# Retention and gated feed-forward on one core: the second product with weights and moving operand exchanged, in four groups over 1024 tokens

## The chip, the core and the metric

The kernel runs on one NeuronCore of a Trainium2 chip. The core has a matrix engine (TensorE, in the profile PE; PEld is its loading of weights), VectorE (DVE), ScalarE (ACT), GpSimd (POOL) and SyncE (SP), on which this kernel issues its DMAs. Each engine has an instruction queue of its own and works through it in order; semaphores connect them. The metric is device time in microseconds (us), from runs on the chip.

## The reference

Inputs are `q`, `k`, `v` (4 batches, 8 heads, 768 steps, 64 dimensions), `w_in` (512 x 2048) and `w_out` (2048 x 512), all float32. First a retention: for each head a 64 x 64 state that decays by `gamma` and takes up one outer product a step.

```python
gamma = 1.0 - 2.0 ** (-5.0 - np.arange(H, dtype=np.float32))
for t in range(S):
    state = gamma[None, :, None, None] * state + np.einsum('bhd,bhe->bhde', k[:, :, t], v[:, :, t])
    y[:, :, t] = scale * np.einsum('bhd,bhde->bhe', q[:, :, t], state)
x = y.transpose(0, 2, 1, 3).reshape(B * S, H * D)      # 3072 tokens x 512
h = x @ w_in
g = h * np.clip(h + 3.0, 0.0, 6.0) / 6.0
out = g @ w_out                                        # 3072 x 512
```

## The kernel before

The program has two stages. **The first** makes `g`. Retention is done in rows of 128 tokens (`burst`, L237) as masked products plus a carried state. Its result `x` is multiplied with `w_in` in `mm1` (L363): one call takes one unit `u` of 512 tokens (`UT`) and one block `jj` of 128 features; 4 pieces of the inner dimension, 3 matmuls each (L368), with the weights from `w_in` and 512 columns of `x` moving. There are three because each float32 operand is kept as two tiles, a high part of type float32r and the rest (`split`, L136: ScalarE copies the high part, VectorE subtracts it), and three of the four cross products are added up. `mm1` ends with ScalarE (L372), VectorE (L373) and a store of `g` to DRAM, transposed, as `gd[jj // 2][:, jj % 2, tokens]` (L374). So `gd[j]` for j = 0..7 holds a pair of feature blocks, one of each half of the features, by 3072 tokens. `w_out` comes in and is made ready in `build_w2` (L165), piece by piece in the first stage; `w2c[j]` holds, for pair j, seven combinations of its four 128 x 256 blocks, each as high and low part and in two halves `h` of 128 output columns.

**The second stage** (L407 on) is the product with `w_out`, as a 2 x 2 block product with seven multiplications in place of eight. The four blocks of `g` are two halves of features (`f`) by two halves of tokens (`t`): a11 and a12 are the first tokens' halves of features, a21 and a22 the second tokens'. Products 1 to 7 take the left operands a11, a12, a12 - s2, a22, s1, s2 and a11 - a21, where s1 = a21 + a22 and s2 = s1 - a11. Twelve blocks `tb` of 256 tokens run one after the other; each has four chunks `cf` of two pairs. Per chunk two loads `gr` from `gd` on SP (L431), four sums of 256 elements on VectorE (L437 to L440), five splits, then 2 pairs x 7 products x 3 matmuls (L454): **weights are 128 tokens of the left operand, 256 columns of `w2c` move**, and the result lies with tokens on the partitions, in four PSUM banks `o`; two sets of banks alternate by block. At a block's end one ScalarE copy and seven VectorE combinations (L469) join the seven products, and one store (L481) writes 256 rows of `out`; the last block has four smaller stores (L485).

What sets the order: in the first stage TensorE's order is the order of the code (`manual_schedule`, L378, closed at L403). All else is ordered by a scheduler, by the order in the code and by what each instruction waits for. The first chunk's preparation has a raised priority and is done early; the other chunks of the first block are put behind the last `g` on VectorE (`issue_after(end)`, L428). Tiles come from pools; a tile taken again waits for its last users.

Of the kernel before, what the change touches and what calls it, by code (L numbers as in the profile page):

```python
# [9 lines left out]
F32 = mybir.dt.float32  # L10
# [14 lines left out]
LEFT = {1: 0, 2: 1, 3: 2, 4: 3, 5: 4, 6: 5, 7: 6}  # L25
# [4 lines left out]
def retention_ffn(ctx: ExitStack, tc: tile.TileContext, qkv, w_in, w_out, dvs, dqs, out, B, H, S, D):  # L30
# [7 lines left out]
    NT, DM = out.shape  # L38
# [47 lines left out]
    def nm(s):  # L86
        return f"{s}_{next(serial)}"
# [315 lines left out]
    order.close()  # L403
# [3 lines left out]
    sets = (late, ctx.enter_context(tc.tile_pool(name="gcpool", bufs=1, reuse_waits="tile")))  # L407
    gpool = ctx.enter_context(tc.tile_pool(name="gpool", bufs=2, reuse_waits="tile"))
# [4 lines left out]
    CF = 2  # L413

    for tb in range(NT // (2 * P)):
        t0 = tb * 2 * P
        banks = [ps_o[tb % 2].tile([P, 512], F32, tag=f"o{i}", name=f"o{tb}_{i}") for i in range(4)]
        acc = {}
        for b_, ids in enumerate(((1, 2), (6, 7), (5, 3), (4,))):
            for n, i in enumerate(ids):  # L420
                acc[i] = (banks[b_][:, n * HM : (n + 1) * HM], n == 0)
        for cf in range(NFP // CF):
            pool = sets[cf % 2]
            with ExitStack() as first:
                if tb == 0 and cf < 1:
                    first.enter_context(tc.high_priority())
                elif tb == 0:
                    first.enter_context(tc.issue_after(end))  # L428
                gv = pool.tile([P, CF, 2, 2, P], F32, tag="gr", name=f"gr{tb}_{cf}", bufs=2)
                for jj in range(CF):  # L430
                    nc.sync.dma_start(  # L431
                        out=gv[:, jj].rearrange("p f t n -> p f (t n)"),
                        in_=gd[cf * CF + jj][:, :, t0 : t0 + 2 * P],
                    )
                a11, a12, a21, a22 = gv[:, :, 0, 0, :], gv[:, :, 1, 0, :], gv[:, :, 0, 1, :], gv[:, :, 1, 1, :]
                sm = pool.tile([P, 4, CF, P], F32, tag="gsum", name=f"gsum{tb}_{cf}")
                dve_add(sm[:, 1], a21, a22)  # L437
                dve_sub(sm[:, 2], sm[:, 1], a11)
                dve_sub(sm[:, 3], a11, a21)
                dve_sub(sm[:, 0], a12, sm[:, 2])  # L440
                gc = pool.tile([P, 2, 7, CF, P], F32R, tag="gc", name=f"gc{tb}_{cf}")
                for i, src in ((0, a11), (1, a12), (3, a22)):
                    split(gc[:, 0, i], gc[:, 1, i], src)
# [115 lines left out]
```

## Time and profile before

| what | value |
|---|---|
| timed runs, median of 3 (lowest to highest) | 601.03 us (600.01 to 602.43) |
| profiled execution, first to last instruction | 597.6 us |
| median of the timed runs less that span | 3.4 us |
| mean granted clock of TensorE | 0.993 |
| matmuls, weight loads | 4988 each |
| read from HBM, written | 71.85 MB, 31.46 MB |

The time of a run is longer than the span of a profiled execution by what lies ahead of its first instruction and behind its last. The page of the profile gives, per engine, busy time as a share of the span, and the span in 40 slices, where a digit is the busy share in tenths. Matmuls overlap, so the mean duration of one is longer than the distance from one to the next. Groups of instructions are told by line, engine and operation, with `out<-in` by the program's names; behind the bar stand busy time, mean duration in ns, and the idle time ahead of them with what ended it. For one line the three numbers are the shortest, middle and longest duration in ns, then the first and last start in us. A DMA row gives its count, the size of one and the middle time from issue to landing.

### The profile page before, as it was taken

The numbers are of one execution on the slowest core, as the hardware profiler recorded it, in microseconds if no ns is written. First come the engines' busy times: TensorE is split into PE (matmuls) and PEld (weight loads), VectorE is DVE, ScalarE is ACT, GpSimd is POOL, SyncE is SP. The second block draws the span as 40 slices with busy tenths as digits, with TensorE's granted clock in tenths as the row PEclk, the third lists the DMA queues.
The fourth block names the chain that finished last, engine by engine and source line by source line (L and its number), as shares of the span: only waits on it lengthen the run. The fifth ranks groups of instructions, "written<-read, shape, count | busy, mean of one in ns | idle before, by whom it ended". The sixth has DMA issues, their size and how long they took to land.

```text
span 597.6 us, 12608 instructions
## 1 busy us (share of the span) xinstructions
PE 580.7 (97%) x4988; PEld 520.3 (87%) x4988; DVE 456.1 (76%) x961; ACT 253.3 (42%) x540; POOL 22.1 (4%) x27
## 2 busy tenths in 40 slices
PE   7698999999999999999999999999999999999997
PEld 6576888877888888888888889999999999999997
DVE  4889999999333797333356969998899889988983
ACT  5774544544222443222244634444444444444441
POOL 1001000010100010001000000000000000000000
PEclk9899999999999999999999999999999999999999
DMA  9976877566745468454244444443444344434411
GB/s 327 390 239 211 259 232 262 200 213 218 241 160 177 159 229 268 171 191 148 106 149 138 171 141 149 142 144 116 128 141 141 119 128 141 142 117 129 142 57 37
DMA packets 64731, 104.13 MB, mean 174 GB/s; under 512 B 5792, under 2 KB 30880, under 8 KB 64672
## 3 DMA queue, kind: packets, MB, share of 16 engines
q1 hardware_dynamic: 64528, 103.31, 51.7%
q8 instruction: 39, 0.64, 0.5%
q14 instruction: 20, 0.16, 0.1%
q10 hardware_dynamic: 144, 0.02, 0.0%
HBM read 71.85 MB, written 31.46 MB: 173 GB/s over the span
## 4 chain that ended last, share of the span: by engine, by line
PE 76%; DVE 17%; DMA 3%; issue 3%; SPq 1%; ACT 0%; DVEq 0%; ACTq 0%
PE o L454 40%; PE h L368 31%; DVE g L373 3%; PE y L269 2%; DVE wb L125 2%; DMA st<-in_w_in 2%; DVE w L138 2%; DVE am L311 2%; DVE we L128 2%; DVE ww L131 1%; PE sc L258 1%; DVE we L119 1%; DVE wb L120 1%; DVE x L138 1%; DVE ws L90 1%
## 5 line engine op out<-in xcount | busy, mean ns | idle before, releaser
L368 PE MATMUL h<-x,w 128*128 128x512 f32 x1152 | 269.9, 392 | 3.8 <-ACT x L137 1.5
L368 PEld LDWEIGHTS h<-x,w 128*128 128x128 f32 x1152 | 214.1, 188 | 52.5 <-DVE x L138 2.5
L454 PEld LDWEIGHTS o<-w,gc 128*128 128x128 f32 x2016 | 239.9, 191 | 0.2
L454 PE MATMUL o<-w,gc 128*128 128x256 f32 x2016 | 240.1, 282 | 0.0
L373 DVE SCALAR_TENSOR_TENSOR g<-g,h 128x512 f32<-128x512 f32 x96 | 65.5, 684 | 83.0 <-ACT g L372 83.0
L372 ACT ACTIVATE g<-h,three 128x512 f32<-128x512 f32 x96 | 65.6, 684 | 102.0 <-PE h L368 97.9
L137 ACT ACTIVATE gc<-gr 128x256 fp32r<-128x256 f32 x144 | 49.6, 407 | 117.6 <-PE o L454 114.2
L138 DVE TENSOR_TENSOR gc<-gr,gc 128x256 fp32r<-128x256 f32 x144 | 52.7, 421 | 20.2 <-ACT gc L137 20.2
L138 DVE TENSOR_TENSOR gc<-gsum,gc 128x768 fp32r<-128x768 f32 x96 | 62.1, 688 | 5.5 <-ACT gc L137 5.5
L137 ACT ACTIVATE gc<-gsum 128x768 fp32r<-128x768 f32 x96 | 54.6, 616 | 0.1
L137 ACT ACTIVATE w<-ww 128x384 fp32r<-128x384 f32 (+2 forms) x34 | 18.7, 555 | 46.5 <-DVE ww L131 44.1
L123 ACT ACTIVATE we<-we,ebias 128x512 int32<-128x512 int32 x32 | 23.0, 718 | 15.2 <-DVE we L119 15.2
L222 POOL TENSOR_TENSOR vn<-vn,cst_sb 128x512 f32<-128x512 f32 x16 | 19.7, 1232 | 260.8 <-DMA vn<-in_qkv 260.8
L311 DVE TENSOR_TENSOR am<-sc,mask 128x1024 f32<-128x1024 f32 x24 | 29.2, 1215 | 0.0
L131 DVE SCALAR_TENSOR_TENSOR ww<-wb,we 128x512 f32<-128x512 f32 x32 | 23.0, 719 | 0.6
L138 DVE TENSOR_TENSOR w<-ww,w 128x384 fp32r<-128x384 f32 (+2 forms) x34 | 19.9, 591 | 2.9 <-ACT w L137 2.8
L125 DVE SCALAR_TENSOR_TENSOR wb<-st,wb 128x512 f32<-128x512 uint32 x32 | 22.0, 686 | 0.2
L128 DVE SCALAR_TENSOR_TENSOR we<-st,we 128x512 int32<-128x512 int32 x32 | 21.9, 685 | 0.1
L93 DVE TENSOR_TENSOR gsum<-gr 128x256 f32<-128x256 f32 x48 | 20.4, 425 | 1.8 <-DMA gr<-gd 0.3
L119 DVE TENSOR_SCALAR we<-st 128x512 int32<-128x512 int32 x32 | 14.3, 446 | 8.5 <-DMA st<-in_w_in 8.3
L90 DVE TENSOR_TENSOR gsum<-gr,gsum 128x256 f32<-128x256 f32 x48 | 20.2, 421 | 0.7
L90 DVE TENSOR_TENSOR gsum<-gr 128x256 f32<-128x256 f32 x48 | 20.1, 418 | 0.0
(51 smaller groups left out, 337.6 us busy)
## 6 DMA issues: line engine op xcount, KB each, us to landing
gd<-g SPq DMA_DIRECT2D x96, 256.0 KB, 2.3
gr<-gd SPq DMA_DIRECT2D x96, 256.0 KB, 3.2
st<-in_w_in SPq DMA_DIRECT2D x16, 512.0 KB, 4.6
st<-in_w_out SPq DMA_DIRECT2D x16, 512.0 KB, 4.1
early<-in_qkv SPq DMA_DIRECT2D x28, 256.0 KB, 6.0
out<-ot SPq DMA_DIRECT2D x11, 512.0 KB, 2.8
kn<-in_qkv SPq DMA_DIRECT2D x16, 256.0 KB, 4.5
kt<-in_qkv SPq DMA_DIRECT2D x16, 256.0 KB, 4.3
```

The costliest lines, as they stand in the source:

```text
L90: return nc.vector.tensor_tensor(out=out_, in0=a, in1=b, op=ALU.subtract)
L123: nc.scalar.activation(out=e, in_=e, func=AF.Relu, scale=8.0, bias=ebias)
L125: nc.vector.scalar_tensor_tensor(out=y, in0=lo.bitcast(U32), scalar=2.0**-32, in1=b, op0=ALU.mult, op1=ALU.add)
L128: nc.vector.scalar_tensor_tensor(out=e, in0=hi, scalar=-2147483648, in1=e, op0=ALU.bitwise_and, op1=ALU.bitwise_or)
L131: nc.vector.scalar_tensor_tensor(out=w, in0=y, scalar=2.0**-20, in1=e.bitcast(F32), op0=ALU.mult, op1=ALU.mult)
L137: nc.scalar.activation(out=hi, in_=src, func=AF.Copy)
L138: nc.vector.tensor_tensor(out=lo, in0=src, in1=hi, op=ALU.subtract)
L311: nc.vector.tensor_tensor(out=new["am"].rearrange("p h a n -> p h (a n)"), in0=sc.rearrange("p h a n -> p h (a n)"), in1=mask.rearrange("p ...
L368: nc.tensor.matmul(h, t[:, o, a], xs[u][b][:, k], start=k + n == 0, stop=(k, n) == (NK - 1, 2), skip_group_check=True)
L372: nc.scalar.activation(out=g, in_=h, func=AF.Relu, bias=three)
L373: ins = nc.vector.scalar_tensor_tensor(out=g, in0=g, scalar=6.0, in1=h, op0=ALU.min, op1=ALU.mult)
L454: nc.tensor.matmul(ps, gc[:, a, LEFT[i], jj, :], wc[:, RIGHT[i], b_], start=first and j == 0 and n == 0, stop=j == NFP - 1 and n == 2, ski ...
```

## The change

The second stage is written anew; the first stays as it is, but all of its line numbers are smaller by one.

- **Operands are exchanged.** The weights of a matmul are now 128 x 128 of `w2c` (product, part, half `h`), and 512 tokens of the left operand move. The result has output columns on the partitions and tokens along the row. `out` is therefore 512 x 3072 in the kernel, and the host turns it back after the run.
- **Blocks of 1024 tokens** (`TB`), two units of 512 as the token halves; three blocks `sb` in place of twelve.
- **Four groups a block**, products (4, 5), (1, 6), (7,) and (2, 3). Each group goes once through the four chunks `c` of two pairs, loads only the quarter or half of `g` that it needs (`gv`), and makes one or two left operands (`gc`, 1024 elements a partition). Block a11 is loaded for groups 2 and 3, and so 1.5 times as many bytes are read. The sums s1 and s2 stay in `spare` from group to group.
- **PSUM**: one tile of two banks per product; two sets alternate by group.
- **Results** are joined as groups end, in five tiles `p`, `q`, `s`, `u`, `v`; two stores after group (7,), two after group (2, 3), of 512 KB each; four of 256 KB at the end of the last block.
- **Buffers**: three `gv` tiles and five `gc` tiles go round. They lie where tiles of the first stage lay.
- **`order.close()`** moves to the end, so TensorE's order is that of the code in the second stage too.

```diff
-    NT, DM = out.shape
+    DM, NT = out.shape
...
-    order.close()
     ph1.close()
...
+    CP = 2
+    TB = 2 * UT
+    GROUPS = ((4, 5), (1, 6), (7,), (2, 3))
+    spare = [place([P, 14 * BLK], F32, f"spare{i}", False) for i in range(2)]
+    sums = [spare[c // 2][:, c % 2 * CP * UT : (c % 2 + 1) * CP * UT].rearrange("p (j n) -> p j n", j=CP) for c in range(4)]
+    kept = {n: spare[i][:, 4 * UT : 6 * UT].rearrange("p (h n) -> p h n", h=2) for i, n in enumerate("su")}
...
+    for sb in range(NT // TB):
+        for g, ids in enumerate(GROUPS):
+            acc = {i: ps_o[g % 2].tile([P, 2, UT], F32, tag=f"o{n}", name=nm("o")) for n, i in enumerate(ids)}
+            for c in range(NFP // CP):
+                with ExitStack() as first:
+                    if sb == 0 and g == 0 and c == 0:
+                        first.enter_context(tc.high_priority())
+                    elif sb == 0 and g == 0:
+                        first.enter_context(tc.issue_after(end))
+                    gv = gv_tile()
+                    for jj in range(CP):
+                        j = c * CP + jj
+                        t0 = 2 * sb * UT
+                        if g == 0:
+                            nc.sync.dma_start(out=gv[:, :, jj], in_=gd[j][:, :, t0 + UT : t0 + TB])
+                        elif g == 2:
+                            src = gd[j][:, 0, t0 : t0 + TB].rearrange("p (t n) -> p t n", t=2)
+                            nc.sync.dma_start(out=gv[:, :, jj], in_=src)
+                        else:
+                            nc.sync.dma_start(out=gv[:, 0, jj], in_=gd[j][:, g // 2, t0 : t0 + UT])
+                    a, b = gv[:, 0], gv[:, 1]
+                    s = sums[c]
+                    if g == 0:
+                        dve_add(s, a, b)
+                        srcs = (b, s)
+                    elif g == 1:
+                        dve_sub(s, s, a)
+                        srcs = (a, s)
+                    elif g == 2:
+                        dve_sub(b, a, b)
+                        srcs = (b,)
+                    else:
+                        dve_sub(s, a, s)
+                        srcs = (a, s)
+                    ops = []
+                    for src in srcs:
+                        gc = gc_tile()
+                        split(gc[:, 0], gc[:, 1], src)
+                        ops.append(gc)
+                for i, gc in zip(ids, ops):
+                    for h in range(2):
+                        for jj in range(CP):
+                            j = c * CP + jj
+                            for n, (x, y) in enumerate(((0, 0), (0, 1), (1, 0))):
+                                nc.tensor.matmul(
+                                    acc[i][:, h],
+                                    w2c[j][:, RIGHT[i], x, h],
+                                    gc[:, y, jj],
+                                    start=j == 0 and n == 0,
+                                    stop=j == NFP - 1 and n == 2,
+                                    skip_group_check=True,
+                                )
+            if g == 0:
+                scaled(kept["p"], acc[4], -SIXTH)
+                scaled(kept["q"], acc[5])
+            elif g == 1:
+                scaled(kept["s"], acc[1])
+                acc6(kept["u"], acc[6], kept["s"])
+                dve_add(kept["v"], kept["u"], kept["q"])
+            elif g == 2:
+                acc6(kept["u"], acc[7], kept["u"])
+                dve_add(kept["p"], kept["u"], kept["p"])
+                dve_add(kept["q"], kept["u"], kept["q"])
+                store(sb, 1, 0, kept["p"], whole)
+                store(sb, 1, 1, kept["q"], whole)
+            else:
...
+                for k, i, m in (("s", 2, 0), ("v", 3, 1)):
+                    for h in parts:
+                        acc6(kept[k][:, h], acc[i][:, h], kept[k][:, h])
+                        store(sb, 0, m, kept[k], h)
+    order.close()
```

In instructions, TensorE's row at the start of the second stage. Before, the first pair of the first chunk (`o_0` to `o_3` are the four banks, `w_188` is `w2c[0]`, `gc_0` the left operands):

```order
L368 MATMUL h_3685<-x_2874,w_173_1280 128x512 x12
L454 MATMUL o_0_3719<-w_188_1381,gc_0_3731 128x256 x6
L454 MATMUL o_1_3720<-w_188_1381,gc_0_3731 128x256 x6
L454 MATMUL o_2_3721<-w_188_1381,gc_0_3731 128x256 x6
L454 MATMUL o_3_3722<-w_188_1381,gc_0_3731 128x256 x3
```

Now, the first chunk (`o_3741` is product 4, `o_3742` product 5; `w_188` and `w_232` are pairs 0 and 1):

```order
L490 MATMUL o_3741<-gc_3747,w_188_1381 128x512 x3
L490 MATMUL o_3741<-gc_3747,w_232_1668 128x512 x3
L490 MATMUL o_3741<-gc_3747,w_188_1381 128x512 x3
L490 MATMUL o_3741<-gc_3747,w_232_1668 128x512 x3
L490 MATMUL o_3742<-gc_3750,w_188_1381 128x512 x3
L490 MATMUL o_3742<-gc_3750,w_232_1668 128x512 x3
```

A product takes 12 matmuls of 512 columns from one operand tile before the next one is touched; before, all seven products took turns at 256 columns. Ahead of this place TensorE's row is the same as before.

SP's queue at the handover. Before (`gr_1` is the second chunk's tile, `g_3698` the last block of `g`):

```order
L374 DMA gd_69<-g_3627 128x512
L374 DMA gd_69<-g_3644 128x512
L374 DMA gd_70<-g_3681 128x512
L431 DMA gr_1_3784<-gd_65 128x2x256
L431 DMA gr_1_3784<-gd_66 128x2x256
L374 DMA gd_70<-g_3698 128x512
```

Now (`gv_3777` and `gv_3811` are the second and third chunk's tiles):

```order
L373 DMA gd_69<-g_3627 128x512
L460 DMA gv_3777<-gd_65 128x2x512
L460 DMA gv_3777<-gd_66 128x2x512
L373 DMA gd_69<-g_3644 128x512
L460 DMA gv_3811<-gd_67 128x2x512
L373 DMA gd_70<-g_3681 128x512
L460 DMA gv_3811<-gd_68 128x2x512
L373 DMA gd_70<-g_3698 128x512
```

The second chunk's loads stand two stores of `g` further ahead, and each is twice as large.

VectorE's queue in the new kernel where group (1, 6) ends and TensorE works on group (7,); `gv_4080` and `gc_4084` belong to the fourth chunk of group (7,), `gv_4106` and `gv_4140` and the `gc` made from them to group (2, 3), and `o_3882` is product 6:

```order
L89 TENSOR_TENSOR gv_4080<-gv_4080 128x1024
L89 TENSOR_TENSOR spare_3736<-gv_4106,spare_3736 128x1024
L137 TENSOR_TENSOR gc_4084<-gv_4080,gc_4084 128x1024
L440 SCALAR_TENSOR_TENSOR spare_3737<-o_3882,spare_3736 128x1024
L137 TENSOR_TENSOR gc_4110<-gv_4106,gc_4110 128x1024
L92 TENSOR_TENSOR kept_v<-spare_3737,kept_q 128x1024
L137 TENSOR_TENSOR gc_4113<-spare_3736,gc_4113 128x1024
```

This has no counterpart before: the combination that waits for product 6 now stands in the middle of the operands of later products, behind the last operand of group (7,) and ahead of the first of group (2, 3).

More of the change, by code (lines that the diff above doesn't have):

```diff
@@ L21 @@
 SIXTH = 1.0 / 6.0
-LEFT = {1: 0, 2: 1, 3: 2, 4: 3, 5: 4, 6: 5, 7: 6}
 RIGHT = {1: 0, 2: 1, 3: 2, 4: 3, 5: 4, 6: 5, 7: 6}
@@ L402, in retention_ffn @@
             advance(UR * (u + 1) + 2 + int((jj + 1) / NF * UR + 0.5))
-    order.close()
     ph1.close()
-    sets = (late, ctx.enter_context(tc.tile_pool(name="gcpool", bufs=1, reuse_waits="tile")))
-    gpool = ctx.enter_context(tc.tile_pool(name="gpool", bufs=2, reuse_waits="tile"))
+    left = {
+        n: ctx.enter_context(tc.tile_pool(name=f"left_{n}", bufs=1, reuse_waits="tile"))
+        for n in ("gv0", "gv1", "gc2", "v", "p", "gc0", "gc1", "q")
+    }
     ps_o = [
@@ new lines, in retention_ffn, with gv_tile @@
+    CP = 2
[4 more added lines that the diff above has]
+    kept = {n: spare[i][:, 4 * UT : 6 * UT].rearrange("p (h n) -> p h n", h=2) for i, n in enumerate("su")}
+    for n in "pqv":
+        kept[n] = left[n].tile([P, 2, UT], F32, name=f"kept_{n}")
+    n_gv, n_gc = 0, 0
+    def gv_tile():
+        nonlocal n_gv
+        pool = (late, left["gv0"], left["gv1"])[n_gv % 3]
+        n_gv += 1
+        return pool.tile([P, 2, CP, UT], F32, tag="gv", name=nm("gv"))
@@ new lines, in gc_tile, with scaled, acc6, store @@
+    def gc_tile():
+        nonlocal n_gc
+        i = n_gc % 5
+        pool = late if i < 2 else left[f"gc{i - 2}"]
+        n_gc += 1
+        return pool.tile([P, 2, CP, UT], F32R, tag=f"gc{i}", name=nm("gc"))
+    def scaled(out_, ps, s=SIXTH):
+        nc.scalar.activation(out=out_, in_=ps, func=AF.Copy, scale=s)
+    def acc6(out_, ps, other):
+        nc.vector.scalar_tensor_tensor(out=out_, in0=ps, scalar=SIXTH, in1=other, op0=ALU.mult, op1=ALU.add)
+    def store(sb, t, m, src, h):
+        o = out[m * HM : (m + 1) * HM, (2 * sb + t) * UT : (2 * sb + t + 1) * UT].rearrange("(h p) n -> p h n", p=P)
+        nc.sync.dma_start(out=o[:, h], in_=src[:, h])
@@ new lines, in retention_ffn @@
+    for sb in range(NT // TB):
[50 more added lines that the diff above has]
+                                )
+            whole = slice(0, 2)
+            if g == 0:
[12 more added lines that the diff above has]
+            else:
+                parts = (whole,) if sb < NT // TB - 1 else (slice(0, 1), slice(1, 2))
+                for k, i, m in (("s", 2, 0), ("v", 3, 1)):
+                    for h in parts:
+                        acc6(kept[k][:, h], acc[i][:, h], kept[k][:, h])
+                        store(sb, 0, m, kept[k], h)
@@ L553 @@
     ]
-    out = nc.dram_tensor("out", (B * S, moe_w_out.shape[1]), F32, kind="ExternalOutput").ap()
+    out = nc.dram_tensor("out", (moe_w_out.shape[1], B * S), F32, kind="ExternalOutput").ap()
     with tile.TileContext(nc) as tc:
@@ L557 @@
     r = run_bass_kernel_spmd(nc, [arrays], core_ids=[0])
-    return r.results[0]["out"]
+    return np.ascontiguousarray(r.results[0]["out"].T)
```

70 lines of the change are left out of this document (removed).

## The prediction

> **What bounds the kernel now.** I read the page from the top: busy time by engine, the slices, the chain that ended last.
>
> ```profile
> span 597.6 us, 12608 instructions
> PE 580.7 (97%) x4988; PEld 520.3 (87%) x4988; DVE 456.1 (76%) x961; ACT 253.3 (42%) x540; POOL 22.1 (4%) x27
> ...
> PE   7698999999999999999999999999999999999997
> ...
> PEclk9899999999999999999999999999999999999999
> ```
>
> TensorE is busy in every slice after the fourth, at full granted clock; no other engine comes near. Busy time does not say how fast the matmuls follow each other, since they overlap. So next: the chain in order of time (start, length, what), where the first product hands over to the second.
>
> ```profile
> 304.81 49.19 PE h L368 x216
> 354.00 66.04 PE o L454 x554
> ```
>
> The chain goes from one product straight into the other with nothing between. The windows give each engine's busy time (and instructions), the granted clock, the DMA engines' busy share and GB/s:
>
> ```profile
> core 0: us, PE busy (x) PEld busy (x) DVE busy (x) ACT busy (x) POOL busy (x), PEclk, DMA share, GB/s
> 400.00:450.00 50.00, 50.00 (x423) 50.00 (x422) 43.20 (x107) 21.59 (x53) 0.00 (x0) 1.00 0.41 130
> 450.00:500.00 50.00, 50.00 (x422) 50.00 (x422) 44.56 (x111) 21.97 (x55) 0.00 (x0) 1.00 0.43 137
> ```
>
> In the second product VectorE is busy 86 to 89%, ScalarE 43%, the DMA engines 41 to 43%. The end of the second product can therefore move only if its matmuls need less time in sum, or if TensorE begins to wait. The pace is read from the first and last start of each matmul line, the two times ahead of the shapes.
>
> ```profile
> L454 PE MATMUL o<-w,gc x2016: 274/281/385, 353.8 to 593.6; 128*128 128x256 f32 x184
> ...
> L368 PE MATMUL h<-x,w x195: 388/389/389, 309.6 to 353.6; 128*128 128x512 f32 x195
> ```
>
> Second product: (593.6 - 353.8) / 2015 = 119.0 ns from one 256-column matmul to the next. First product, its last stretch where no attention work lies between: (353.6 - 309.6) / 194 = 226.8 ns for 512 columns. Twice 119.0 is 238.0. So 512 columns in one matmul cost 11.2 ns less than in two: each matmul has a part of about 11 ns that doesn't depend on its width.
>
> **The change part by part.** *Matmuls.* 12 blocks x 8 x 7 x 3 = 2016 of 256 columns become 3 blocks x 7 products x 2 halves x 8 x 3 = 1008 of 512 columns. Columns in sum are the same. The new ones have the shape, the types and the 128x128 weights of L368, one weight load each, so I take its 226.8 ns. They start where the old ones start, at 353.8, because everything ahead on TensorE is unchanged. Last start: 353.8 + 1007 x 0.2268 = 582.2; with its 0.389 it ends at 582.6. Before, the last one ended at 593.6 + 0.28 = 593.9. **Gain 11.3 us.**
>
> [...]
>
> *VectorE and ScalarE.* The same elements are prepared in wider instructions of 1024. Their durations don't stand in this trace; these bound them:
>
> ```profile
> L138 DVE TENSOR_TENSOR gc<-gr,gc 128x256 fp32r<-128x256 f32 x141 | 51.5, 421 | 20.2 <-ACT gc L137 20.2
> L137 ACT ACTIVATE gc<-gr 128x256 fp32r<-128x256 f32 x141 | 48.5, 407 | 116.7 <-PE o L454 114.2 <-DMA gr<-gd 2.5
> L138 DVE TENSOR_TENSOR gc<-gsum,gc 128x768 fp32r<-128x768 f32 x47 | 45.0, 957 | 5.5 <-ACT gc L137 5.5
> L137 ACT ACTIVATE gc<-gsum 128x768 fp32r<-128x768 f32 x47 | 39.0, 829 | 0.1
> ```
>
> On VectorE 512 more elements cost 957 - 421 = 536 ns, so 1024 last 957 + 268 = 1.23 us. On ScalarE 829 + 211 = 1.04 us. A block of 1024 tokens has 44 such adds and subtracts plus 7 for the results: 51 x 1.23 = 63 us of VectorE, and 28 + 3 copies: 32 us of ScalarE. TensorE needs 336 x 0.2268 = 76.2 us for the block. VectorE falls to 82% and stays off the bound in sum. If it alone set the pace it would be 63 us a block, so this costs nothing as long as TensorE's operands are ready ahead.
>
> *How far ahead.* Five operand tiles go round; while TensorE works on one (12 matmuls, 2.72 us), up to four are ready, a cover of 10.9 us. The new wait is in VectorE's queue: the combination of product 6 (`spare_3737<-o_3882`) waits until group (1, 6) has ended, and the operands of group (2, 3) are queued behind it. By then the four operands of group (7,) are made (the row just ahead of it is the fourth), so TensorE has those 10.9 us while VectorE needs 1.2 to combine and 1.2 for the next operand. Cost nothing. The group (7,) itself is the tight one: 8 preparing instructions and 3 for its results, 11 x 1.23 = 13.5 us of VectorE against 10.9 of TensorE; the 2.6 us come out of the cover and are won back in group (2, 3), where 12 + 2 instructions (17.2 us) stand against 21.8.
>
> *The handover at 354.*
>
> ```profile
> 354.76 0.69 DVE L373 SCALAR_TENSOR_TENSOR g<-g,h 128x512 f32<-128x512 f32 x1 [2.03 <-ACT g L372]
> 355.36 0.42 DVE L93 TENSOR_TENSOR gsum<-gr 128x256 f32<-128x256 f32 x1
> ```
>
> Chunk 0 is prepared in advance. Chunk 1 of the new order begins on VectorE at 355.4, behind the last `g`: the sum (1.2) and the first operand's subtract (1.2) are done by 357.9. TensorE asks for it after 24 matmuls, at 353.8 + 5.4 = 359.2. Its loads are queued on SP behind the store of `g_3627`, two `g` stores earlier than those of chunk 1 before. So no gap, with 1.3 us to spare; if the loads or the sum slip by more than that, the excess is a gap once.
>
> *Loads.*
>
> ```profile
> L431 SPq DMA_DIRECT2D gr<-gd x96: 517/522/2047, 305.1 to 566.1; - x96
> ...
> gr<-gd SPq DMA_DIRECT2D x96, 256.0 KB, 3.2
> st<-in_w_in SPq DMA_DIRECT2D x16, 512.0 KB, 4.6
> early<-in_qkv SPq DMA_DIRECT2D x28, 256.0 KB, 6.0
> ...
> DMA to landing us min/median/max: 2.8/6.0/7.7
> ```
>
> Still 96 loads, but a block now reads 8 x (512 + 256 + 512 + 256) KB = 12.6 MB, 37.7 MB in all against 25.2. With 6.3 MB of output that is 44 MB in 229 us, 192 GB/s against 130. No engine waits for a load directly. A `gv` tile's trip is two issues of 0.52 on SP (1.0), landing, the sum, the copy and the subtract (1.2 + 1.0 + 1.2): 4.4 us plus landing, and up to three VectorE instructions of the chunk ahead in the queue (3.7). For the landing I take the 512 KB row, 4.6: 12.7 us. Three tiles go round and TensorE takes a chunk every 76.2 / 16 = 4.76 us, so 14.3 us are allowed. Hidden, with 1.6 us to spare. The lower end is `gr`'s 3.2, the upper the 6.0 (at worst 7.7) of the loads at the program's start.
>
> *The tail.*
>
> ```profile
> L469 DVE SCALAR_TENSOR_TENSOR ot<-o,ou x3: 415/425/425, 593.2 to 594.3; 128x256 f32<-128x256 f32 x3
> L485 SPq DMA_DIRECT2D out<-ot x4: 332/344/387, 591.2 to 594.8; - x4
> ...
> gd<-g SPq DMA_DIRECT2D x96, 256.0 KB, 2.3
> out<-ot SPq DMA_DIRECT2D x4, 128.0 KB, 1.7
> ```
>
> Before: matmuls end 593.9, last combination ends 594.7, last store issued 594.8, landed 596.5, span ends 597.6. After: matmuls end 582.6, a combination of 512 columns (0.69, L373's row) ends 583.3, its store of 256 KB (2.3 by `gd<-g`) lands at 585.7, and the same 1.1 us close: 586.8. The tail is 4.2 us instead of 3.7; from 3.7 to 5 seems possible.
>
> **Sum.** 11.3 - 0.5 = 10.8 us less: span 586.8. The median of the timed runs, 601.03, is 3.4 above the profiled span; with the same 3.4 the time is **590.2 us**.
>
> **The rivals.**
>
> *The cover wears out (VectorE).* Each operand is copied by ScalarE, then its rest is made by VectorE, which in the second product waited for those copies (us in all, times):
>
> ```profile
>   ACT gc L137: 25.7, 55
> ```
>
> That is 0.47 us each. If each of the 84 new operands brought such a wait, VectorE would need 153 x 1.23 + 84 x 0.47 = 228 us, as long as TensorE's 229. Group (7,) would then lose 2.6 + 4 x 0.47 = 4.5 us to VectorE, three times. Two operands ready at its start (5.4 us) pay for that; with one (2.7 us) it costs 3 x 1.8 = 5.4 us, 595.6; with none 13.5 us, 603.7. Against it: VectorE's queue puts sums of other chunks between copy and subtract, and begins each group four operands ahead.
>
> *The loads become the bound (slower).* Place: the trip of a `gv` tile. Point: landing over 4.6 + 1.6 = 6.2 us. At the 7.7 of the early loads the trip is 15.8 us, a chunk every 5.27 instead of 4.76: 48 x 0.51 = 24 us, 590.2 + 24 = 614. For it: group (7,) asks for 4.19 MB in 10.9 us, 385 GB/s, as much as the best slice of the page:
>
> ```profile
> DMA  9976877566745468454244444443444344434411
> GB/s 327 390 239 211 259 232 262 200 213 218 241 160 177 159 229 268 171 191 148 106 149 138 171 141 149 142 144 116 128 141 141 119 128 141 142 117 129 142 57 37
> ```
>
> Against it: those loads are issued while group (1, 6), which asks for half per time, is running; the early 6.0 us belong to slices with DMA engines 90% busy, and here the mean would be 0.42 x 192 / 130 = 0.62. [...]
>
> *The fixed part doesn't shrink.* If the second product's 11 ns come from something else than the number of matmuls, for example from the change of accumulator, 512 columns cost up to 238.0 ns there, nothing is gained, and the longer tail makes it 601.5. Against it: L368 has the same shape and the same weight loads and shows 226.8. [...]
>
> That the change doesn't do what it says is excluded by the order of instructions: 1008 matmuls of 128x512 stand there.
>
> **How the numbers follow.** Forecast 590.2, own range 588 to 592.5 (pace 225.5 to 228.5 is 1.6 us either way; tail -0.5 to +0.8): 0.72. Under 588, if the new matmuls go faster than L368's: 0.02. Cover wears to about one operand, 592.5 to 598: 0.11; wholly, 598 to 603.7: 0.05. Fixed part stays, 601.5: 0.03. Loads, 604 to 614: 0.07. A measurement of this kernel tells about 0.5% from no change, so 598.0 and 604.0 are the limits: faster 0.72 + 0.02 + 0.11 = 0.85, same 0.05 + 0.03 = 0.08, slower 0.07. The range 588 to 597.5 leaves out 0.17.
>
> **What would show it.** Right: the second product's matmuls start at 353.8 and 227 ns apart, no gap in TensorE's row, last start near 582, 1024-element VectorE instructions near 1.23 us, landings under 5 us, 4 us from the last matmul to the end. Wrong: TensorE waiting for `gc` from VectorE at the start of groups (2, 3) (the cover) or in every chunk behind loads of over 6 us (the loads); a gap of a few us near 359 (the handover); a pace over 230 ns without waits (the fixed part).

## The result, and the profile after

| | kernel before | changed kernel |
|---|---|---|
| timed runs, median of 4 (lowest to highest), us | 601.73 (600.01 to 602.59) | 594.16 (593.11 to 596.46) |
| ratio of the times, 95% interval | 1 | 0.9879 (0.9843 to 0.9914) |
| profiled execution, first to last instruction, us | 597.6 | 593.0 |
| second product, first start to last end, us | 240.1 | 230.7 |
| last matmul's end to the end of the span, us | 3.7 | 5.2 |
| mean granted clock of TensorE | 0.993 | 0.991 |

The kernel became 7.6 us faster (5.2 to 9.4 by the interval). 10.8 us had been predicted, and a time of 590.2 us; the 594.16 us lie within 588 to 597.5, but above the 588 to 592.5 that the prediction gave to its own account.

The page of the changed kernel, first its busy times and then TensorE's, VectorE's, the clock's and the DMA engines' rows of the slices:

```profile
span 593.0 us, 10098 instructions
PE 573.1 (97%) x3980; PEld 470.9 (79%) x3980; DVE 425.6 (72%) x600; ACT 246.2 (42%) x381; POOL 20.1 (3%) x27
...
PE   6788999999999999999999999999999999999996
...
DVE  4969999999533498333434997869776698766971
...
PEclk9889999999999999999999999999999999999999
DMA  8956677665864458445433547574664757636611
```

TensorE still sets the end: it is busy in every slice after the fourth but the last, at a granted clock of 0.9 or more. How much work the other engines have left is read from the windows, with the columns of before (busy us and instructions of each engine, granted clock, DMA share, GB/s):

```profile
core 0: us, PE busy (x) PEld busy (x) DVE busy (x) ACT busy (x) POOL busy (x), PEclk, DMA share, GB/s
400.00:450.00 50.00, 50.00 (x220) 41.07 (x219) 40.99 (x36) 20.10 (x19) 0.00 (x0) 1.00 0.58 191
450.00:500.00 50.00, 50.00 (x221) 41.04 (x220) 40.32 (x35) 21.98 (x21) 0.00 (x0) 1.00 0.62 200
```

36 wide instructions of VectorE stand where 107 stood, and it is busy 81 to 82% of the time instead of 86 to 89%; the share of the DMA engines went from 0.41 and 0.43 to about 0.6. The weight loads, before back to back (50 of 50 us), now leave 9 us free.

Then the pace, from the lines of the two products (shortest, middle and longest duration in ns, first and last start in us):

```profile
L367 PE MATMUL h<-x,w x196: 389/389/389, 312.8 to 357.0; 128*128 128x512 f32 x196
...
L490 PE MATMUL o<-gc,w x1008: 387/389/398, 357.2 to 587.5; 128*128 128x512 f32 x168
```

The first product keeps its pace: (357.0 - 312.8) / 195 = 226.7 ns. The second has the same shape, and takes (587.5 - 357.2) / 1007 = **228.7 ns**. The waits in the second product (engine and line, what it waited for: us in all, times, longest) show no wait of TensorE at all; these are the ones that the prediction spoke of:

```profile
engine line waited for: us in total, times, longest us
ACT gc L136 <- PE o L490: 95.0, 60, 2.0
DVE gc L137 <- ACT gc L136: 22.1, 20, 1.7
DVE spare L440 <- PE o L490: 8.6, 1, 8.6
DVE spare L89 <- DMA gv<-gd: 7.8, 7, 1.6
DVE gv L89 <- DMA gv<-gd: 7.6, 10, 2.0
DVE spare L92 <- DMA gv<-gd: 7.1, 7, 2.8
...
ACT gc L136 <- DMA gv<-gd: 3.4, 2, 2.5
```

So the 2 ns that a matmul of the second product takes longer are no wait for an operand. The only long wait of a combination (8.6 us) stands at the very end, where VectorE has nothing else to do. The end itself, as a timeline (start, length, engine and instruction, idle time before it):

```profile
585.20 1.29 DVE L440 SCALAR_TENSOR_TENSOR spare<-o,spare 128x512 f32<-128x512 f32 x2 [8.63 <-PE o L490]
585.92 0.94 SPq L444 DMA_DIRECT2D out<-spare  x2
587.92 1.29 DVE L440 SCALAR_TENSOR_TENSOR kept_v<-o,kept_v 128x512 f32<-128x512 f32 x2 [1.43 <-PE o L490]
588.64 1.08 SPq L444 DMA_DIRECT2D out<-kept_v  x2
```

The last product's two halves are combined one behind the other, 1.29 us for both, and only after the last matmul of all (587.9), though the first half had its last matmul six matmuls earlier. Whether the first half's combination could have lain beside those six is what the run best tries below.

**The account of the two executions.** The second product became 240.1 - 230.7 = 9.4 us shorter, the tail (last matmul's end to the end of the span) 5.16 - 3.73 = 1.4 longer. That is 8.0 us, against 7.6 between the medians. The spans themselves differ by 4.6 only, since the second product starts at 357.2 here and at 353.8 in the profile of before, with the same instructions ahead of it on TensorE. Before the second product the kernels of this study differ in nothing that TensorE executes, and their profiles begin it anywhere from 353.8 to 358.8. In the changed kernel's four runs the span goes with the clock:

```
run us   span us   mean granted clock
593.11   591.4     0.997
593.54   591.8     0.994
594.78   593.0     0.991
596.46   594.7     0.985
```

A run is 1.7 to 1.8 us longer than its own span. With that, the profiled execution of before was a run of about 599.4 us, below each of its four timed runs: its 353.8 is the earliest start of all, and not the usual one.

In these four runs the lower clock has the longer span. Over more runs that doesn't hold: of w256's ten, one of 601.7 us had a clock of 0.997 and one of 600.2 us had 0.991. The time at a lower clock can be found in the trace (start and end of the stretch in us, its length, then busy times, granted clock, DMA share and GB/s):

```profile
25.70:28.90 3.20, 3.20 (x50) 3.07 (x52) 3.13 (x6) 1.68 (x5) 0.00 (x0) 0.50 1.04 394
32.50:35.70 3.20, 3.20 (x9) 2.43 (x9) 2.43 (x5) 1.32 (x4) 0.00 (x0) 0.50 0.21 76
```

The changed kernel's profile has three such stretches at half clock before 40 us (the first from 12 to 15 us), that of before has two. Its second product begins 3.4 us later, and the profiles with two stretches alone begin it anywhere from 353.8 to 356.2. So the clock can be at most a part of it, and the cause of the different starts stays open.

### The profile page after: what moved, and what is told of

It is laid out like the page before. It is cut to its first block, busy times and chain, and to the rows that moved or that the text cites. A ratio compares the mean times of both kernels' runs of the same rounds, so it can differ in the third digit from the quotient of the medians.

```text
span 593.0 us, 10098 instructions
## 1 busy us (share of the span) xinstructions
PE 573.1 (97%) x3980; PEld 470.9 (79%) x3980; DVE 425.6 (72%) x600; ACT 246.2 (42%) x381; POOL 20.1 (3%) x27
## 4 chain that ended last, share of the span: by engine, by line
PE 76%; DVE 17%; issue 2%; DMA 2%; ACT 0%; SPq 0%; DVEq 0%; ACTq 0%
PE o L490 39%; PE h L367 31%; PE y L268 3%; DVE g L372 3%; DVE am L310 2%; DVE wb L124 2%; DVE w L137 2%; PE sc L257 2%; DMA st<-in_w_in 2%; DVE we L127 2%; DVE ww L130 2%; DVE we L118 1%; DVE wb L119 1%; DVE ws L89 1%; PE y L244 1%
## 5 line engine op out<-in xcount | busy, mean ns | idle before, releaser
L490 PE MATMUL o<-gc,w 128*128 128x512 f32 x1008 | 230.7, 391 | 0.0
L490 PEld LDWEIGHTS o<-gc,w 128*128 128x128 f32 x1008 | 189.2, 188 | 41.3
L136 ACT ACTIVATE gc<-gv 128x1024 fp32r<-128x1024 f32 x48 | 50.9, 1061 | 62.3 <-PE o L490 55.1
L137 DVE TENSOR_TENSOR gc<-gv,gc 128x1024 fp32r<-128x1024 f32 x48 | 58.6, 1220 | 16.0 <-ACT gc L136 16.0
L136 ACT ACTIVATE gc<-spare 128x1024 fp32r<-128x1024 f32 x36 | 38.2, 1062 | 48.0 <-PE o L490 39.9
L137 DVE TENSOR_TENSOR gc<-spare,gc 128x1024 fp32r<-128x1024 f32 x36 | 43.9, 1220 | 7.3 <-ACT gc L136 7.0
L136 ACT ACTIVATE w<-ww 128x384 fp32r<-128x384 f32 (+2 forms) x34 | 18.7, 555 | 47.7 <-DVE ww L130 45.2
L221 POOL TENSOR_TENSOR vn<-vn,cst_sb 128x512 f32<-128x512 f32 x16 | 17.7, 1105 | 266.5 <-DMA vn<-in_qkv 229.1
L89 DVE TENSOR_TENSOR gv<-gv 128x1024 f32<-128x1024 f32 x12 | 14.7, 1225 | 7.6 <-DMA gv<-gd 7.6
L92 DVE TENSOR_TENSOR spare<-gv 128x1024 f32<-128x1024 f32 x12 | 14.7, 1223 | 7.1 <-DMA gv<-gd 7.1
L89 DVE TENSOR_TENSOR spare<-spare,gv 128x1024 f32<-128x1024 f32 x12 | 14.7, 1221 | 7.1 <-DMA gv<-gd 7.1
```

The lines of the kernel that those rows point to most:

```text
L89: return nc.vector.tensor_tensor(out=out_, in0=a, in1=b, op=ALU.subtract)
L136: nc.scalar.activation(out=hi, in_=src, func=AF.Copy)
L137: nc.vector.tensor_tensor(out=lo, in0=src, in1=hi, op=ALU.subtract)
L490: nc.tensor.matmul(acc[i][:, h], w2c[j][:, RIGHT[i], x, h], gc[:, y, jj], start=j == 0 and n == 0, stop=j == NFP - 1 and n == 2, skip_grou ...
```

## The experiments

The open question was where 1.9 us of the second product and 1.0 us of the tail had gone, and whether the covers on which the prediction rested (operand tiles, loads) were what kept TensorE fed. From here on, the time of a second product is last start - first start of its matmul line (239.8 us before, 230.3 in the changed kernel), and its pace is that divided by (count - 1). Times come with the median of the kernel before on the same chip, or with its one run there.

### w256: twice as many matmuls of half the width

Everything of the changed kernel stays, but each matmul of 512 columns is made as two of 256.

```diff
+ for q in range(0, UT, 256):
...
-     acc[i][:, h], w2c[j][:, RIGHT[i], x, h], gc[:, y, jj],
+     acc[i][:, h, q : q + 256], w2c[j][:, RIGHT[i], x, h], gc[:, y, jj, q : q + 256],
...
```

> The changed kernel with each of its 1008 matmuls of 512 columns cut into two of 256 (same weights loaded twice, same order, same tiles). Fixed-part theory: each matmul has a part of about 11 ns that its width doesn't change, so 2016 matmuls follow each other every 119.0 ns as in the kernel before, the second product takes 239.9 us instead of 230.7, the run about 9 us longer than the changed kernel's. Rival (the gain comes from groups, buffers or the order, not from the number of matmuls): the second product stays near 231 us.

Measured: 603.42 us (10 runs) against 602.06 (14), ratio 1.0018 (1.0007 to 1.0028). Its matmul line:

```profile
L491 PE MATMUL o<-gc,w x2016: 277/283/290, 357.1 to 597.2; 128*128 128x256 f32 x184
```

240.1 us at 119.2 ns, within 0.3 us of what the kernel before needs. Exchanged operands, blocks of 1024, four groups, half as many VectorE instructions: none of it is worth anything on TensorE's path. **The whole gain comes from the number of matmuls**, and the longer tail turns the rest into a small loss. The rival "the fixed part doesn't shrink" falls. In every run each matmul brings a weight load of its own (1008 loads to 1008 matmuls in the changed kernel), also where two of them use the same weights as here (2016 to 2016). So no run tells whether the fixed part belongs to the matmul or to its weight load.

### pad, low and rot: where the operand tiles lie

The starts of single matmuls in the changed kernel's trace show that the loss isn't spread evenly. By the five operand tiles that go round, the mean distance between starts is 230.3, 228.9, 230.8, 226.7 and 226.7 ns, the same to 0.1 ns in each turn, though what goes on beside them varies: in three windows of 11 us from 390 to 423 VectorE was busy for 7.6 to 11.0 us, ScalarE for 4.25 to 5.28, and the DMA share was 0.35 to 0.87. Tiles 0 and 1 lie in the pool `late`, 2 to 4 where `left` is. A pool is a stretch of the on-chip memory; `late` is its upper part. By the addresses of the compiled programs, tiles in `late` begin 96 bytes past a multiple of 128, and those in `left`, the weights `w2c`, and the first product's weights and `x` all 32 bytes past one. Candidates were that offset, the upper part of the memory as such, and contention with what is written there at the same time.

*pad* puts a small tile of 64 bytes into `late` (and one tiny instruction that writes it), so that tiles 0 and 1 come to lie at 32 too; place in the rotation, neighbours and all transfers stay.

```diff
+ if sb == 0:
+     pad = late.tile([P, 16], F32, tag="pad", name="pad")
+     nc.vector.tensor_scalar(out=pad, in0=kept["p"][:, 0, 0:16], scalar1=0.0, scalar2=None, op0=ALU.mult)
```

> The changed kernel with a 64-byte tile added to the pool that holds two of the five operand tiles, so that these two begin 32 bytes past a multiple of 128 like the other three, instead of 96 bytes (one VectorE instruction of 16 elements is added). Offset theory (the 1.9 ns by which a matmul in the second product is slower than in the first come from operands at 96 bytes): all matmuls 226.8 ns apart, second product 228.6 us instead of 230.7. Rival, the place in the upper part of SBUF: no change, 228.7 ns. Rival, contention with VectorE, ScalarE or DMA: no change, 228.7 ns.

*low* takes the load tiles into `late` and all five operand tiles into `left`.

```diff
- pool = (late, left["gv0"], left["gv1"])[n_gv % 3]
+ i = n_gv % 3
...
- return pool.tile([P, 2, CP, UT], F32, tag="gv", name=nm("gv"))
+ return late.tile([P, 2, CP, UT], F32, tag=f"gv{i}", name=nm("gv"))
...
- pool = late if i < 2 else left[f"gc{i - 2}"]
+ pool = left[("gc0", "gc1", "gv0", "gv1", "gc2")[i]]
```

> The changed kernel with tiles exchanged: all five operand tiles in the lower pools, the three load tiles in the upper pool. Offset theory and upper-part theory both: 226.8 ns apart, second product 228.6 us, run about 2 us shorter than the changed kernel's. Contention: no change, 228.7 ns.

*rot* leaves the places and changes the turn in which they are used: 96, 32, 96, 32, 32.

```diff
- pool = late if i < 2 else left[f"gc{i - 2}"]
+ pool = (late, left["gc0"], late, left["gc1"], left["gc2"])[i]
```

> The changed kernel with the five operand tiles in another rotation: upper, lower, upper, lower, lower instead of upper, upper, lower, lower, lower. If the operand's own place is what counts, matmuls of the first and third operand of each five are slow (about 229 ns or more) and those of the last are at 226.7; if it were a matter of the period of five products, the first three in a row stay slow as in the changed kernel.

The matmul line of the second product, first in pad, then in low, then in rot:

```profile
L490 PE MATMUL o<-gc,w x1008: 388/389/389, 358.8 to 587.0; 128*128 128x512 f32 x168
```

```profile
L490 PE MATMUL o<-gc,w x1008: 387/389/496, 355.5 to 584.1; 128*128 128x512 f32 x168
```

```profile
L490 PE MATMUL o<-gc,w x1008: 387/392/503, 355.7 to 587.4; 128*128 128x512 f32 x168
```

64 bytes bring pad to 228.2 us, 226.7 ns by its single starts, the first product's pace. One run of it took 594.32 us because its second product began at 358.8, the latest of all; from there to its span's end it needs 592.6 - 358.8 = 233.8 us, where the changed kernel needs 235.8. low has 228.6 us, and here the time of a run shows it: 590.97 us (4 runs) against 602.06, ratio 0.9812 (0.9797 to 0.9827), an interval wholly below the changed kernel's. (0.3 of its 228.6 us are a short wait between its first three matmuls.) rot goes the other way, 231.7 us (0.3 of them are waits of the same kind at its second and third operand), 593.96 in one run. The same numbers by tile, without distances over 300 ns, in which TensorE waits:

```
          offset of the tiles        mean distance of starts by tile, ns
changed   96  96  32  32  32         230.3  228.9  230.8  226.7  226.7
rot       96  32  96  32  32         230.3  230.8  230.3  230.9  226.7
pad       32  32  32  32  32         226.7  226.7  226.7  226.7  226.7
```

The upper part of the memory and the contention fall, since pad keeps both. A tile at 32 right behind one at 96 is slow as well, which none of the candidates had foreseen; with more changes between the two kinds, rot has more slow tiles. The single starts of the changed kernel show what a change does: in the tile at 32 behind one at 96, ten of the twelve matmuls follow at 224 to 236 ns, and the last two are back at 226 to 227.

### shift and off: an absolute offset, an offset against the weights, or the mixture

*shift* puts the 64 bytes ahead of everything: weights, `x` and all operand tiles lie at 96. *off* puts them ahead of the tiles in `left` alone: all five operand tiles at 96, the weights at 32.

```diff
  # shift, at the head of the kernel
+ pad = const.tile([P, 16], F32, name="pad")
+ nc.gpsimd.memset(pad, 0.0)
...
  # off, ahead of the pools of `left`; the write stands in block sb == 0
+ lpad = ctx.enter_context(tc.tile_pool(name="lpad", bufs=1, reuse_waits="tile")).tile([P, 16], F32, name="lpad")
...
+ nc.vector.tensor_scalar(out=lpad, in0=kept["p"][:, 0, 0:16], scalar1=0.0, scalar2=None, op0=ALU.mult)
```

> The changed kernel with a 64-byte tile added ahead of all others, so that the weights of both products, all operand tiles and x begin 96 bytes past a multiple of 128. If an operand's own offset counts: all operands of the second product slow, about 230 ns, and the first product's matmuls too (there 226.7 before). If it is the offset against the weights: all at 226.7, in both products.

> A 64-byte tile ahead of the tiles in the lower half moves three of the five operand tiles by 64 bytes, so that all five lie 96 bytes past a multiple of 128, while the weights stay 32 bytes past one. Theory A, that what counts is the offset of the moving operand against the weights: every matmul is slow, 229 to 231.5 ns apart in the second product, first to last start 230.6 to 233 us, so about 594 us. Theory B, that what counts is that operand tiles of two offsets take turns: 226.7 ns apart, 228.3 us, about 590.5 us.

The matmul line of shift, then of off:

```profile
L492 PE MATMUL o<-gc,w x1008: 388/389/389, 355.9 to 584.1; 128*128 128x512 f32 x168
```

```profile
L491 PE MATMUL o<-gc,w x1008: 388/392/397, 356.2 to 586.7; 128*128 128x512 f32 x168
```

shift: 228.2 us, 226.7 ns, 591.25 us in one run against 600.23, and its first product, with weights and `x` at 96 too, keeps its pace. off: 230.5 us, 228.9 ns at every tile, 593.29 in one run against 601.09. So 96 is as good as 32 where the weights lie at 96 too, and five like tiles are slow where the weights lie 64 bytes off. **What counts is the offset of the moving operand against the weights.** off came out just under the 229 that had been expected for this (228.9), since the 230.3 to 230.9 of the changed kernel and of rot belong to tiles at a change from one kind to the other, of which off has none.

### w256pad and beforepad: the same at 256 columns

*w256pad* is w256 with the tile of pad. *beforepad* is the kernel before with such a tile in its pool `late`, in which every second of its left operands lies (there they are the weights, at 96, and `w2c` at 32 moves); with it all lie at 32.

```diff
  # beforepad, in the first block
+ pad = late.tile([P, 16], F32, tag="pad", name="pad")
+ nc.vector.tensor_scalar(out=pad, in0=u4[:, 0:16], scalar1=0.0, scalar2=None, op0=ALU.mult)
```

> The kernel w256 (every matmul of the second product cut into two of 256 columns) with the 64-byte tile of pad. If the offset costs something per column or per 256-column matmul too, the pace falls from 119.16 ns to 117.2 to 118.2 (2 to 4 us less); if at 256 columns the weight load, and not the moving operand, sets the pace, it stays at 119.0 to 119.2 and the time at about 603 us.

> The kernel before, with a 64-byte tile added to the pool in which part of its left operands lie (weights there), moved from 96 to 32 bytes past a multiple of 128. If the offset of weights against moving operand costs the kernel before something too, its 119.0 ns fall to 117.5 to 118.5 and the time by 1 to 3 us, and the gain of the change was measured against a kernel that paid the same price; if not, 119.0 stays and the time is within 1 us of the kernel before.

The matmul line of w256pad, then of beforepad:

```profile
L491 PE MATMUL o<-gc,w x2016: 278/283/283, 354.8 to 596.6; 128*128 128x256 f32 x184
```

```profile
L454 PE MATMUL o<-w,gc x2016: 278/283/387, 355.6 to 597.5; 128*128 128x256 f32 x184
```

Neither expectation holds. Both become **slower**: 241.8 us (120.0 ns) instead of 240.1, and 241.9 us (120.1 ns) instead of 239.8. One run each, 603.56 and 603.25 us against 601.09, says little by itself; the paces say it. At 256 columns the differing offset gains 0.8 to 1.1 ns a matmul on average over the tiles, at 512 it costs 2.0. By the single starts of w256 and of before, it is the tiles at 96 themselves that are faster: 117.8 to 117.9 ns there, 120.0 to 120.2 at 32. So the same 64 bytes take 2.2 ns off a matmul of 256 columns and put 2.2 on one of 512 (off). With equal offsets the numbers become simple: 120.0 for 256 columns, 226.7 for 512. That is 106.7 ns for 256 columns (0.417 each) and a fixed part of 120.0 - 106.7 = **13.3 ns per matmul**. Two widths always lie on one line; a third is the next run.

### w128: narrower still

As w256, with four matmuls of 128 columns.

```diff
+ for q in range(0, UT, 128):
...
+     acc[i][:, h, q : q + 128], w2c[j][:, RIGHT[i], x, h], gc[:, y, jj, q : q + 128],
...
```

> The changed kernel with each matmul of 512 columns cut into four of 128. Fixed-part theory (11.2 ns a matmul and 0.421 ns a column, whatever the width): 65 ns from one to the next, 4032 of them 262 us, 31 us more than the changed kernel. Rival, weight loads were already the limit at 256 columns (their row was busy without a break there): they can't follow closer than about 119 ns, 480 us, 250 us more. In between: a load limit under 119 ns, which the pace then shows.

Its row of the weight loads on the page (busy us, mean ns, idle us ahead), and its matmul line, then a window:

```profile
L491 PEld LDWEIGHTS o<-gc,w 128*128 128x128 f32 x4032 | 450.4, 192 | 0.1
```

```profile
L491 PE MATMUL o<-gc,w x4032: 223/275/280, 356.7 to 806.8; 128*128 128x128 f32 x192
```

```profile
400.00:450.00 50.00, 50.00 (x450) 50.00 (x450) 19.21 (x17) 12.16 (x12) 0.00 (x0) 1.00 0.29 96
```

813.77 us in one run, 450.1 us for 4032 matmuls: 111.7 ns each, where columns and fixed part would give 53 + 13 = 67. So the line through 256 and 512 columns doesn't reach down to 128; something else sets the pace there. The weight loads are the likely limit: one for each matmul, 0.1 us idle in 450. That row alone doesn't show it, since the weight loads of w256 are busy without a break too (50.00 of 50 us from 400 to 450), at 119.2 ns. No run changes the weight loads without the matmuls.

### gc3 and gv2: the two covers

*gc3* lets three operand tiles go round in place of five; *gv2* two load tiles in place of three.

```diff
- i = n_gc % 5
+ i = n_gc % 3
```

```diff
- pool = (late, left["gv0"], left["gv1"])[n_gv % 3]
+ pool = (late, left["gv0"])[n_gv % 2]
```

> The changed kernel with three operand tiles in place of five, so at most two are ready while TensorE works on one: cover 5.4 us in place of 10.9. By the prediction's reckoning two ready operands pay for what group (7,) lacks: TensorE waits for nothing, second product near 231 us. Rival (the cover is used up at group ends, where combinations stand in VectorE's queue): TensorE waits at most of the 11 group ends, 1 to 3 us each, second product 240 to 260 us.

> Two load tiles go round in place of three. By the prediction's sum a tile's trip is 12.7 us, so two tiles bring a chunk every 6.35 us where TensorE takes one every 4.8: 48 x 1.55 = 74 us more, about 668 us, with TensorE waiting for operands in every group. If the up to three VectorE instructions of the chunk ahead (3.7 us) that the sum put into the trip do not stand there, the trip is 4.4 + 4.8 = 9.2 us, a chunk every 4.6: within 3 us of the changed kernel. In between would tell how much of the queue counts.

gc3's matmul line, then what its TensorE waited for in the second product:

```profile
L490 PE MATMUL o<-gc,w x1008: 387/392/505, 357.2 to 590.1; 128*128 128x512 f32 x168
```

```profile
PEld o L490 <- DVE gc L137: 1.8, 3, 0.9
PE o L490 <- DVE gc L137: 0.5, 1, 0.5
```

597.16 us in one run against 600.23; the second product takes 232.9 us, 2.6 more than the changed kernel's. By the single starts, six distances above 300 ns lose 1.3 us in sum, all at the first matmuls of the fourth operand of a group (7,): the place that the prediction called the tight one. The other 1.3 are no waits: two of the three tiles left lie at 96, and the mean of the changed kernel's first three (230.0) is 1.3 ns above its mean over five, over 1007 matmuls. So two tiles ahead (5.4 us) almost suffice, as the prediction had it, and the fourth and fifth tile are spare but for these 1.3 us.

gv2's matmul line, and the waits for loads in its second product:

```profile
L490 PE MATMUL o<-gc,w x1008: 387/389/398, 357.5 to 587.8; 128*128 128x512 f32 x168
```

```profile
ACT gc L136 <- DMA gv<-gd: 18.7, 8, 3.4
DVE spare L89 <- DMA gv<-gd: 10.8, 11, 2.5
...
DVE gv L89 <- DMA gv<-gd: 9.1, 6, 2.2
...
DVE spare L92 <- DMA gv<-gd: 4.2, 5, 1.1
```

594.34 us in one run against 601.09, and 230.3 us of second product as with three. VectorE's waits for loads grow from 22.5 us (7.8 + 7.6 + 7.1) to 24.1 and ScalarE's from 3.4 to 18.7, but TensorE waits for nothing. The prediction's trip of 12.7 us would have cost 74 us here. Two tiles and a chunk every 4.76 us leave 9.5 us for a trip on average, so the 3.7 us of "VectorE instructions of the chunk ahead" can't all belong to every trip.

### best: low with the last product's halves apart

The last half of the last product gets a PSUM tile of its own, so that the combination of the first half needn't wait for the second's matmuls.

```diff
+ half = {i: [a[:, h] for h in range(2)] for i, a in acc.items()}
+ if sb == NT // TB - 1 and g == len(GROUPS) - 1:
+     half[3][1] = ps_o[0].tile([P, 2, UT], F32, tag="o1", name=nm("o"))[:, 0]
...
-     acc[i][:, h],
+     half[i][h],
```

> The kernel with operand tiles in the lower pools, and with the second half of product 3 in the last group in a PSUM tile of its own, so that the first half's combination needn't wait for the last matmul. Tail theory (0.6 us of the 5.1 us from the last matmul to the end are a second 512-column combination in series): the end comes 0.6 to 0.9 us sooner after the last matmul, 4.2 to 4.5 us; matmuls 226.7 ns apart; run about 590.3 us, 8 us under the changed kernel's distance to before plus 3: ratio to before near 0.980. If the wait is for something else, the tail stays 5.1 us.

The timeline of its end:

```profile
584.64 0.69 DVE L440 SCALAR_TENSOR_TENSOR kept_v<-o,kept_v 128x512 f32<-128x512 f32 x1
585.35 1.69 SPq L444 DMA_DIRECT2D out<-kept_v  x2
586.00 0.69 DVE L440 SCALAR_TENSOR_TENSOR kept_v<-o,kept_v 128x512 f32<-128x512 f32 x1 [0.67 <-PE o L493]
```

The first half is combined at 584.6, while the matmuls run, and the second 1.4 us later, right behind the last matmul (585.6 + 0.4). From there to the span's end at 589.6 it takes 3.7 us: as short as before (3.7) and shorter than the 4.2 to 4.5 that had been expected, where the profiles of kernels with the tail of the change and 512 columns need 4.4 (gv2, low, off, rot) to 5.2 (pad). 590.67 us (6 runs) against 600.23 (11), ratio 0.9837 (0.9813 to 0.9860). It is faster than the kernel before. Against low, measured on another chip, its 0.3 us tell nothing, and the two intervals overlap; that the tail is shorter is read from the profile alone.

## Why the prediction was right, and where its sizes were wrong

- **What bounds the kernel, and that the number of matmuls is the gain: right.** w256 shows it, by taking the gain back with all else left as changed.
- **The time: within 588 to 597.5, in part by luck.** 594.16 us lie above the 588 to 592.5 that had 0.72, in the 592.5 to 598 that the prediction gave to a worn cover of operands. That isn't what happened: TensorE waits for no operand. The pace and the tail both came just beyond what the account allowed (228.7 ns against 228.5, 5.2 us against 5.0), and the profile of before was an early one; the next points take these up.
- **"So I take its 226.8 ns": mis-sized, 1.9 us.** The pace was 228.7. Shape, types and weight loads were the same, as the step said; the offset of the operands against each other was not, and pad and shift reach 226.7 with the same matmuls in the same order. With equal offsets the second product takes 228.2 + 0.4 = 228.6 us, a gain of 240.1 - 228.6 = 11.5 where 11.3 was predicted.
- **"A part of about 11 ns": right as a mechanism, and by luck near in size.** It was worked out from a line with differing offsets (119.0) and one with equal ones (226.8). Like with like it is 13.3 (w256pad against pad) or 2 x 119.2 - 228.7 = 9.7 (w256 against the changed kernel).
- **Tail "4.2 us instead of 3.7": mis-sized, 1.0 us in this profile, 0.2 to 1.0 in the others.** The sum had one combination behind the last matmul. There are two, 0.6 us more, and the last store is issued behind the second; best takes that away. What makes the same tail 4.4 us in one profile and 5.2 in another stays open.
- **"With the same 3.4 the time is 590.2": right in form, but 1.6 of the 3.4 were the luck of the profiled execution**, as every run is only 1.7 to 1.8 us longer than its own span. As a difference of medians the prediction was 10.8; 7.6 came, and by the profile 1.9 + 1.0 = 2.9 of the 3.2 that are missing are the two terms above. The rest is within what medians of four runs tell.
- **VectorE 1.23 and ScalarE 1.04 us at 1024 elements: right**, as the page's rows of the copy and the subtract show (behind the first bar: busy us, then mean ns of one):

```profile
L136 ACT ACTIVATE gc<-gv 128x1024 fp32r<-128x1024 f32 x48 | 50.9, 1061 | 62.3 <-PE o L490 55.1
L137 DVE TENSOR_TENSOR gc<-gv,gc 128x1024 fp32r<-128x1024 f32 x48 | 58.6, 1220 | 16.0 <-ACT gc L136 16.0
```

- **The cover of 10.9 us and the wait for product 6: right.** VectorE waited for copies for 22.1 us instead of the 39 (84 x 0.47) that the first rival needed, and for the combination of product 6 not at all: by the time it stands there, the group has ended. With three tiles in place of five the waits cost 1.3 us (gc3), so the cover was ample.
- **The handover: right.** VectorE's row there, in the changed kernel:

```profile
358.12 0.69 DVE L372 SCALAR_TENSOR_TENSOR g<-g,h 128x512 f32<-128x512 f32 x1 [1.71 <-ACT g L371]
358.73 1.22 DVE L92 TENSOR_TENSOR spare<-gv 128x1024 f32<-128x1024 f32 x1
359.87 1.22 DVE L137 TENSOR_TENSOR gc<-gv,gc 128x1024 fp32r<-128x1024 f32 x1
```

The first operand of the second chunk is done at 361.1, and TensorE asks for it at 357.2 + 24 x 0.2287 = 362.7: 1.6 us to spare, where 1.3 were predicted.

- **Loads hidden: right, but the margin of 1.6 us was mis-sized.** The landing came as taken:

```profile
gv<-gd SPq DMA_DIRECT2D x48, 512.0 KB, 4.8
gv<-gd SPq DMA_DIRECT2D x48, 256.0 KB, 3.1
```

4.8 us for the large ones (4.6 predicted), and only 3.1 for the half of them that bring 256 KB, which the sum had left out. Two tiles would have done (gv2), so a trip of 12.7 us was too long; without the queue of VectorE the sum is 4.4 + 4.8 = 9.2 us against 14.3 allowed. The 385 GB/s that the prediction set against group (7,) never came. Here are the windows while the first such group runs (the second line) and beside it:

```profile
390.10:401.10 11.00, 11.00 (x49) 9.02 (x49) 7.60 (x7) 5.28 (x5) 0.00 (x0) 1.00 0.73 250
401.10:412.10 11.00, 11.00 (x50) 9.02 (x49) 11.00 (x11) 4.25 (x4) 0.00 (x0) 1.00 0.35 101
412.10:423.00 10.90, 10.90 (x49) 8.95 (x48) 9.71 (x9) 4.25 (x4) 0.00 (x0) 1.00 0.87 297
```

With three tiles most of the group's loads come while the group ahead still runs. VectorE is busy for all of the 11 us, so the group is as tight for it as the prediction said.

## What to carry to other kernels

Where a chain of matmuls is the bound and nothing waits, count the matmuls: here 13.3 ns went with each one of 256 or 512 columns and its weight load, on top of 0.417 ns a column (w256pad against pad), and wide moving operands pay that less often. A pace taken over from another line of the same kernel was good to 1% here; that last 1% hung on where the operands lay, and moving tiles by 64 bytes took 2.1 us off (pad, 228.2 us against 230.3). The halves of the last result, read one by one, needed a tile each; in one tile both waited for the last matmul (4.4 us from its end to the end of the span in low, 3.7 with two tiles in best).

## What the runs showed that was not expected

- **The pace of a matmul depends on the offset of the moving operand against the weights.** Both at 32, or both at 96 bytes past a multiple of 128: 226.7 ns at 512 columns; both at 32: 120.0 at 256. 64 bytes apart: 228.9 at 512, 230.3 to 230.9 in tiles at a change from one kind to the other. At 256 columns it is faster 64 bytes apart, 117.8 to 117.9. Only this one distance of 64 bytes was tried, and the cause of the slower and of the faster pace stays open, as does why a tile with the right offset is slow behind one with the wrong.
- **At 128 columns a matmul and its weight load take 111.7 ns** (w128), not the 67 of the line through 256 and 512 columns. That the weight load is the limit is likely and not shown.
- **The second product begins up to 4.9 us earlier or later** (353.8 to 358.8 in 14 profiles), with the same work ahead of it on TensorE. The kernels differ elsewhere, but spans of the kernel before alone lie between 597.6 and 601.8 us, on two chips. A profile's absolute times should be compared from a common point in the program, as the second product's start here, and not from the span's.
